# PSUM shared out anew in a fused Fourier and expert kernel: double banks for the Fourier stages, two single banks for the W_in products

## The chip, the cores and the metric

The kernel runs on one core of a Trainium2 chip, as one launch. The metric is device time in microseconds: the median over runs of the whole program, here three of them.

## What is computed

Eight sequences of 3008 tokens with 256 features pass through a Fourier layer and then a wide product layer:

```python
X = np.fft.rfft(x, axis=1)                        # x: 8 x 3008 x 256
Yr = Xr @ w_r - Xi @ w_i + b_r
Yi = Xr @ w_i + Xi @ w_r + b_i                    # w_r, w_i: 256 x 256
Yr, Yi = soft-threshold by 0.01
x = np.fft.irfft(Yr + 1j * Yi, n=3008, axis=1)
h = x @ w_in                                      # w_in: 256 x 2048
out = (h * np.cos(h)) @ w_out                     # w_out: 2048 x 256
```

## The kernel before

The transform over 3008 = 64 x 47 tokens is done as matrix products: `stage_a` multiplies by a 64-point transform, `stage_b` by a 47-point one (`f2t1`), then by the Fourier weights (`wmix`, split into high and low fp32r parts), then `fold` and `spread` go back over the 47 points, and `stage_c` back over the 64 and splits the result into `xTh` and `xTl`. Between stages the data goes through DRAM scratch: `scr1` behind `stage_a`, `scrT` inside `fold`, `scr2` behind `spread`. In `stage_a` (L365) and `spread` (L544) the matmuls are 64x64, four of them to a group, which differ in the 64 rows (`h`) and the 64 columns (`v`) of the array that they use; the two with one `h` write one bank. Such a group is called a quartet below.

The expert layer runs as tiles of 512 tokens, 6 per batch, with 16 steps per tile. A step (`moe_step`) makes a 128x512 block of h with six matmuls into `ph` (L678 to L680), then takes it through a chain: ScalarE rounds h / 2 pi (L685), VectorE subtracts (L686), ScalarE takes the sine (L688), VectorE multiplies by h (L689), ScalarE casts to `gh` (L690), and the rest `gl` is subtracted on GpSimd or VectorE by turns (L267, L270). `ph` is read by L685, L686 and L689. Three steps later `second` multiplies `gh` and `gl` by W_out with six matmuls (L660, L661, L664) into the accumulators `o0` and `o1`.

Batch b's expert steps run beside the Fourier stages of batch b + 1 and `stage_a` of batch b + 2: `moe_step` calls `pull` twice, which draws pieces from these generators according to the costs that they yield (`A_PAIR`, `F2_COST`, and so on). The order in which each engine takes its instructions is then set by a planner that simulates the program as it lays it out; on the chip each engine's order is fixed. Batch 0's Fourier stages run alone ahead of all this, in a prologue that also loads and splits the weights; the splitting of W_out goes on in the first tile.

PSUM has eight banks of 512 fp32 columns. Before, three single banks have the tag `f` (all Fourier work), three the tag `h` (`ph`), and `o0` and `o1` have one each. In the prologue the Fourier stages take turns over all eight.

Of the kernel before, what the change touches and what calls it, by code (L numbers as in the profile page):

```python
# [39 lines left out]
A_EVERY, A_FIRST = 7, 13  # L40
A_PAIR = 1.06
# [99 lines left out]
def tile_body(ctx: ExitStack, tc, x, w_r, w_i, b_r, b_i, w_in, w_out,  # L141
# [78 lines left out]
    def split_f64(hi, lo, raw):  # L220
# [3 lines left out]
        m = wk.tile([128, 512], F32, tag="tr", name="wm", bufs=2)  # L224
# [51 lines left out]
    def fps(name):  # L276
        if "pro" in pool:
            if not banks:
                banks.extend(("f", "h", "o0", "f", "h", "o1", "f", "h"))
            tag = banks.pop(0)  # L280
            return ps.tile([128, 512], F32, tag=tag, name=name, bufs=1 if tag[0] == "o" else 3)
        return ps.tile([128, 512], F32, tag="f", name=name, bufs=3)

    def stage_in(name):
        return wk.tile([128, 512], F32, tag="xt", name=name, bufs=4)

    def stage_out(name):
        return wk.tile([128, 512], F32, tag="ao", name=name, bufs=3)
# [54 lines left out]
    def stage_a(b):  # L343
# [13 lines left out]
        for cc in range(6):  # L357
            for v in range(2):
                load(2 * cc + 2 + v)
            p = [fps("pa") for _ in range(2)]  # L360
            xs = [ld.pop(2 * cc + v) for v in range(2)]
            for v in range(2):
                for h in range(2):
                    hs = slice(64 * h, 64 * h + 64)
                    mm(p[h][64 * v:64 * v + 64], ff[hs, 256:], xs[v][hs], start=True, stop=True, skip_group_check=True)  # L365
            for h in range(2):
                ao = stage_out("ao")
                nc.scalar.copy(ao, p[h])
                for v in range(2):
                    i = 4 * cc + 2 * v  # L370
                    nc.sync.dma_start(scr1[b][:, :, h, i:i + 2].rearrange("s r i d -> (s r) (i d)"), ao[64 * v:64 * v + 64])
            yield A_PAIR


    def stage_b(b):
# [26 lines left out]
        def f2t1(q):  # L402
            if b == 0:
                xf = wk.tile([128, 3, 2, 8, 48], F32, tag=("Xh", "Xl")[q % 2], name="Xf", bufs=1)
                X[q] = xf
            else:
                xh = wk.tile([128, 3, 2, 8, 48], F32R, tag="Xh", name="Xh", bufs=1)
                xl = wk.tile([128, 3, 2, 8, 48], F32R, tag="Xl", name="Xl", bufs=1)
                X[q] = (xh, xl)
            for hf in range(4):  # L410
# [11 lines left out]
                if b:  # L422
                    at = ld.pop(u)
                    p = fps("pb")
# [404 lines left out]
```

## Time and profile before

| | |
|---|---|
| time, median of 3 runs | 2778.85 us (2776.76 to 2781.24) |
| profiled execution, its own time | 2778.31 us |
| its span, first to last instruction | 2776.5 us |
| mean granted TensorE clock | 0.994 |
| busy: TensorE, VectorE, ScalarE, GpSimd | 99%, 65%, 61%, 36% |

The span is what the trace covers; the time of the run has some 1.8 us around it. Busy shares are over the whole span. PE is TensorE, DVE is VectorE, ACT is ScalarE, POOL is GpSimd, SP is SyncE, which issues most of the DMAs.

### The profile page before, as it was taken

To read this page: it belongs to the slowest core of one execution; us is meant where nothing else is said; L and a number is where in the kernel's file an instruction comes from. 1 tells how busy PE (TensorE), PEld (TensorE's weight loads), DVE (VectorE), ACT (ScalarE), POOL (GpSimd) and SP (SyncE) were. 2 spreads that over 40 slices of the span, in tenths; PEclk is the share of its full clock that TensorE was granted. 3 is DMA by queue.
4 is the path that set the end of the run, shared out by engine and by line. 5 is a ranking of instruction groups with operands and counts; after the bars stand their busy time and mean duration, and the time that the engine had idled before them with its cause. 6 is when DMAs were issued, how large, how long until landed. Compare 5 with 4: busy or idle time off the path is not lost.

```text
span 2776.5 us, 36936 instructions
## 1 busy us (share of the span) xinstructions
PE 2741.0 (99%) x13161; PEld 2192.4 (79%) x13161; DVE 1808.6 (65%) x2856; ACT 1690.0 (61%) x3020; POOL 989.6 (36%) x907
## 2 busy tenths in 40 slices
PE   8799999999999999999999999999999999999999
PEld 6487778877788777887778777788777888888888
DVE  6586675766657666676666766667665666666665
ACT  5575556655665655655656555665556656566666
POOL 4354432443324442244322534224442343322222
PEclk9899999999999999999999999999999999999999
DMA  6522333133311433123331233212333122121000
GB/s 188 152 79 73 103 105 91 49 104 111 101 58 54 111 112 101 41 73 107 100 94 42 75 107 105 84 48 73 103 113 92 30 73 88 58 57 38 16 16 15
DMA packets 151193, 224.95 MB, mean 81 GB/s; under 512 B 16976, under 2 KB 94304, under 8 KB 151008
## 3 DMA queue, kind: packets, MB, share of 16 engines
q1 hardware_dynamic: 145728, 205.26, 25.5%
q0 software_dynamic: 5280, 17.33, 2.0%
q8 instruction: 104, 1.70, 0.3%
q14 instruction: 81, 0.66, 0.1%
HBM read 121.33 MB, written 101.19 MB: 80 GB/s over the span
## 4 chain that ended last, share of the span: by engine, by line
PE 93%; DMA 3%; DVE 2%; ACT 0%; SPq 0%; issue 0%; POOL 0%; ACTq 0%; POOLq 0%; DVEq 0%
PE ph L678 12%; PE po L661 12%; PE po L660 12%; PE ph L679 12%; PE ph L680 12%; PE po L664 12%; PE pi L544 3%; PE pb L428 3%; PE pc L641 3%; PE pa L365 2%; PE pw L474 2%; PE pw L473 2%; PE pw L472 2%; DMA y<-scrT 1%; DMA scrT<-tr 1%; PE pw L468 0%
## 5 line engine op out<-in xcount | busy, mean ns | idle before, releaser
L267 POOL TENSOR_TENSOR gl<-u,gh 128x512 fp32r<-128x512 f32 (+1 forms) x384 | 489.1, 1274 | 1301.3 <-ACT gh L690 1086.1
L686 DVE SCALAR_TENSOR_TENSOR u<-ph,u 128x512 f32<-128x512 f32 (+1 forms) x768 | 518.6, 675 | 449.0 <-ACT u L685 447.2
L689 DVE TENSOR_TENSOR u<-ph,u 128x512 f32<-128x512 f32 (+1 forms) x768 | 519.7, 677 | 295.4 <-ACT u L688 279.6
L688 ACT ACTIVATE u<-u 128x512 f32<-128x512 f32 (+1 forms) x768 | 480.1, 625 | 329.1 <-DVE u L686 327.5
L685 ACT ACTIVATE u<-ph 128x512 int32<-128x512 f32 (+1 forms) x768 | 451.2, 588 | 302.1 <-PE ph L680 294.9
L678 PE MATMUL ph<-xTh,win 128*128 128x512 f32 (+1 forms) x1536 | 615.3, 401 | 1.2 <-ACT xTh L645 0.7
L690 ACT CAST gh<-u 128x512 fp32r<-128x512 f32 (+1 forms) x768 | 467.8, 609 | 243.9 <-DVE u L689 242.1
L660 PE MATMUL po<-gh,wout 128*128 128x512 f32 (+1 forms) x1536 | 603.5, 393 | 0.7 <-ACT gh L690 0.7
L661 PE MATMUL po<-gh,wout 128*128 128x512 f32 (+1 forms) x1536 | 599.5, 390 | 0.0
L679 PE MATMUL ph<-xTl,win 128*128 128x512 f32 (+1 forms) x1536 | 597.7, 389 | 0.0
L680 PE MATMUL ph<-xTh,win 128*128 128x512 f32 (+1 forms) x1536 | 597.5, 389 | 0.0
L664 PE MATMUL po<-gl,wout 128*128 128x512 f32 (+1 forms) x1536 | 476.2, 388 | 0.0
L270 DVE TENSOR_TENSOR gl<-u,gh 128x512 fp32r<-128x512 f32 (+1 forms) x384 | 329.4, 858 | 98.3 <-ACT gh L690 95.9
L678 PEld LDWEIGHTS ph<-xTh,win 128*128 128x128 f32 x1536 | 289.8, 189 | 80.2 <-issue 20.3
L661 PEld LDWEIGHTS po<-gh,wout 128*128 128x128 f32 x1536 | 288.9, 188 | 80.9 <-issue 33.3
L660 PEld LDWEIGHTS po<-gh,wout 128*128 128x128 f32 x1536 | 288.9, 188 | 74.5 <-issue 21.9
L680 PEld LDWEIGHTS ph<-xTh,win 128*128 128x128 f32 x1536 | 289.0, 188 | 68.0 <-issue 13.8
L679 PEld LDWEIGHTS ph<-xTl,win 128*128 128x128 f32 x1536 | 289.8, 189 | 65.0 <-issue 19.5
L664 PEld LDWEIGHTS po<-gl,wout 128*128 128x128 f32 x1536 | 285.9, 188 | 58.0 <-issue 3.2
L641 PEld LDWEIGHTS pc<-ff,bt 128*128 128x128 f32 x768 | 112.0, 193 | 24.1 <-issue 13.4
L428 PEld LDWEIGHTS pb<-f,at 96*128 96x128 f32 x896 | 121.0, 191 | 10.3 <-DVE Xl L433 0.2
L641 PE MATMUL pc<-ff,bt 128*128 128x128 f32 x768 | 113.3, 277 | 12.6 <-DMA bt<-scr 12.6
(111 smaller groups left out, 2494.8 us busy)
## 6 DMA issues: line engine op xcount, KB each, us to landing
scrT<-tr SPq DMA_DIRECT2D x56, 512.0 KB, 2.7
y<-scrT SPq DMA_DIRECT2D x112, 256.0 KB, 5.0
bt<-scr SPq DMA_DIRECT2D x96, 256.0 KB, 3.7
xt<-in_dram SPq DMA_DIRECT2D x84, 256.0 KB, 3.2
scr<-ao SPq DMA_DIRECT2D x168, 128.0 KB, 2.9
at<-scr SPq DMA_DIRECT2D x112, 192.0 KB, 2.8
scr<-bo SPq DMA_DIRECT2D x224, 96.0 KB, 2.0
out_dram<-ob SPq DMA_DIRECT2D x80, 256.0 KB, 2.2
```

The source lines that it names most:

```text
L267: return nc.gpsimd.tensor_tensor(out=lo, in0=x, in1=hi.bitcast(F32), op=ALU.subtract)
L660: mm(po[e][:, :n], wo[0][:, 0, f, es], gh[:, :n], start=f == 0, stop=False)
L661: mm(po[e][:, :n], wo[0][:, 1, f, es], gh[:, :n], start=False, stop=False)
L664: mm(po[e][:, :n], wo[0][:, 0, f, es], gl[:, :n], start=False, stop=f == NFC - 1)
L678: mm(h, win[:, 0, c, fs], th[:, c, :n], start=c == 0, stop=False)
L679: mm(h, win[:, 0, c, fs], tl[:, c, :n], start=False, stop=False)
L680: mm(h, win[:, 1, c, fs], th[:, c, :n], start=False, stop=c == 1)
L685: nc.scalar.activation(k[:, :n], h, AF.Identity, bias=0.25, scale=1.0 / TWO_PI)
L686: nc.vector.scalar_tensor_tensor(out=u[:, :n], in0=h, scalar=1.0 / TWO_PI, in1=k[:, :n], op0=ALU.mult, op1=ALU.subtract)
L688: nc.scalar.activation(u[:, :n], u[:, :n], AF.Sin, bias=HALF_PI, scale=TWO_PI)
L689: nc.vector.tensor_tensor(out=u[:, :n], in0=h, in1=u[:, :n], op=ALU.mult)
L690: nc.scalar.copy(gh[:, :n], u[:, :n])
```

## The change

PSUM is divided anew: the tag `f` becomes two tiles of two banks each (`pair`), `h` has two single banks instead of three, `o0` and `o1` stay. In the steady part every Fourier product goes into a pair and is evicted over both banks at once: `stage_a`, `f2t1`, `wmix` (which now makes both halves e of a product together) and `stage_c`; `spread` still copies bank by bank. The four matmuls of a quartet are issued by `burst`, the first with high priority and the others queued directly behind it. `Xh` and `Xl` are laid out so that the wide evictions write in one stretch, and the weights' products read them with gaps. Staging tiles for stores are twice as wide and have half as many DMAs; `xt` has six buffers instead of four, and `tr`, `wm`, `k1`, `cl` (one instead of two) and `yf` (two instead of four) have fewer. In `wmix` both calls of `fold` stand behind the last product. The costs and rates that the generators are drawn by are set to the new pieces.

```diff
 GAP = 5
-A_EVERY, A_FIRST = 7, 13
-A_PAIR = 1.06
+A_EVERY, A_FIRST = 3, 13
+A_PAIR = 1.15
 SPREAD, SPREAD_FIRST = 1.2, 1.1
 
...
         a = wk.tile([128, 512], F32, tag="t2", name="wa", bufs=1)
         q = wk.tile([128, 512], F32, tag="t1", name="wq", bufs=1)
...
+        if not banks:
+            banks.extend(("f", "h", "o0", "f", "h", "o1"))
+        tag = banks.pop(0)
+        if tag == "f":
+            return pair(name)[:, 0]
+        return ps.tile([128, 512], F32, tag=tag, name=name, bufs=1 if tag[0] == "o" else 2)
+
+    def pair(name):
+        return ps.tile([128, 2, 512], F32, tag="f", name=name, bufs=2)
+
+    def burst(calls):
+
+        with tc.high_priority():
+            ins = mm(*calls[0][0], **calls[0][1])
+            with tc.issue_after(ins.ins):
+                for a, k in calls[1:]:
+                    mm(*a, **k)
 
     def stage_in(name):
-        return wk.tile([128, 512], F32, tag="xt", name=name, bufs=4)
+        return wk.tile([128, 512], F32, tag="xt", name=name, bufs=6)
 
     def stage_out(name):
-        return wk.tile([128, 512], F32, tag="ao", name=name, bufs=3)
+        return wk.tile([128, 1024], F32, tag="ao", name=name, bufs=3)
...
         for cc in range(6):
+            p = pair("pa")
+            xs = [ld.pop(2 * cc + v) for v in range(2)]
+            burst([((p[64 * v:64 * v + 64, h], ff[64 * h:64 * h + 64, 256:], xs[v][64 * h:64 * h + 64]),
+                    dict(start=True, stop=True, skip_group_check=True)) for v in (1, 0) for h in range(2)])
+            ao = stage_out("ao")
+            nc.scalar.copy(ao, p.rearrange("p h x -> p (h x)"))
             for v in range(2):
+                i = 4 * cc + 2 * v
+                nc.sync.dma_start(scr1[b][:, :, :, i:i + 2].rearrange("s r g i d -> (s r) g (i d)"),
+                                  ao[64 * v:64 * v + 64].rearrange("p (g x) -> p g x", g=2))
                 load(2 * cc + 2 + v)
-            p = [fps("pa") for _ in range(2)]
-            xs = [ld.pop(2 * cc + v) for v in range(2)]
-            for v in range(2):
-                for h in range(2):
-                    hs = slice(64 * h, 64 * h + 64)
-                    mm(p[h][64 * v:64 * v + 64], ff[hs, 256:], xs[v][hs], start=True, stop=True, skip_group_check=True)
-            for h in range(2):
-                ao = stage_out("ao")
-                nc.scalar.copy(ao, p[h])
-                for v in range(2):
-                    i = 4 * cc + 2 * v
-                    nc.sync.dma_start(scr1[b][:, :, h, i:i + 2].rearrange("s r i d -> (s r) (i d)"), ao[64 * v:64 * v + 64])
             yield A_PAIR
...
-                xh = wk.tile([128, 3, 2, 8, 48], F32R, tag="Xh", name="Xh", bufs=1)
-                xl = wk.tile([128, 3, 2, 8, 48], F32R, tag="Xl", name="Xl", bufs=1)
-                X[q] = (xh, xl)
+                xyh = wk.tile([128, 2304], F32R, tag="Xh", name="Xh", bufs=1)
+                xyl = wk.tile([128, 2304], F32R, tag="Xl", name="Xl", bufs=1)
+                xh, xl = (m[:, :1536].rearrange("p (s g k) -> p s g k", s=8, g=4) for m in (xyh, xyl))
+                yh, yl = (m[:, 1536:].rearrange("p (c s k) -> p c s k", c=2, s=8) for m in (xyh, xyl))
+                X[q] = tuple([[m[:, :, 2 * r + c].rearrange("p s k -> p s k") for c in range(2)] for r in range(2)]
+                             + [[n[:, c] for c in range(2)]] for m, n in ((xh, yh), (xl, yl)))
...
-                    p = fps("pb")
-                    pv = p[:, :384].rearrange("p (s r c k) -> p s r c k", s=2, r=2, c=2)
+                    if hf % 2 == 0:
+                        p = pair("pb")
+                    pv = p[:, hf % 2, :384].rearrange("p (s r c k) -> p s r c k", s=2, r=2, c=2)
                     for j in range(2):
                         for c in range(2):
                             mm(pv[:, j, :, c], at[:, j, 128 * c:128 * c + 128], f2[:, 2 * (hf % 2) + j],
                                start=j == 0 and c == 0, stop=j == 1 and c == 1, skip_group_check=True)
-                    pv = p[:, :384].rearrange("p (s g k) -> p s g k", s=2, g=4)
-                    xhv, xlv = (a[:, :2].rearrange("p r c s k -> p s (r c) k")[:, 2 * hf:2 * hf + 2] for a in (xh, xl))
+                    if hf % 2 == 0:
+                        continue
+                    pv = p[:, :, :384]
+                    xhv, xlv = (a[:, 2 * hf - 2:2 * hf + 2].rearrange("p (u s) g k -> p u (s g k)", u=2) for a in (xh, xl))
                     nc.scalar.copy(xhv, pv)
                     nc.vector.tensor_tensor(out=xlv, in0=pv, in1=xhv.bitcast(F32), op=ALU.subtract)
-                    yield 2 * F2_COST
+                    yield 4 * F2_COST
...
+                (xhr, xhi), (xlr, xli) = ([m.bitcast(F32).rearrange("p s (r c) k -> p r c s k", r=2)[:, r] for r in range(2)]
+                                        for m in (xh, xl))
+                po.tensor_tensor(out=t1, in0=xhr, in1=xhi, op=ALU.add)
+                nc.scalar.copy(yh, t1)
+                po.tensor_tensor(out=t2, in0=xlr, in1=xli, op=ALU.add)
+                po.tensor_tensor(out=t1, in0=t1, in1=yh.bitcast(F32), op=ALU.subtract)
+                po.tensor_tensor(out=yl, in0=t1, in1=t2, op=ALU.add)
...
+            if b:
+                k1 = wk.tile([128, 2, 8, 48], F32, tag="k1", name="k1", bufs=1)
+                for wj, comp in ((0, 2), (1, 0), (2, 1)):
+                    p = pair("pw")
+                    for e in range(2):
+                        es = slice(128 * e, 128 * e + 128)
+                        for c in range(2):
+                            xhv, xlv = (x[comp][c] for x in xs)
+                            mm(p[:, e, :384], wf[:, wj, 0, c, es], xhv, start=c == 0, stop=False)
+                            mm(p[:, e, :384], wf[:, wj, 1, c, es], xhv, start=False, stop=False)
+                            mm(p[:, e, :384], wf[:, wj, 0, c, es], xlv, start=False, stop=c == 1)
+                    p4 = p[:, :, :384].rearrange("p e (s k) -> p e s k", k=48)
+                    if wj == 0:
+                        nc.scalar.copy(k1, p4)
+                        yield 2.0
+                        continue
+                    r = 2 - wj
+                    sv = st[:, :, :, r, :]
+                    if r:
+                        nc.vector.tensor_tensor(out=sv, in0=p4, in1=k1, op=ALU.add)
+                    else:
+                        nc.vector.tensor_tensor(out=sv, in0=k1, in1=p4, op=ALU.subtract)
+                    cl = wk.tile([128, 2, 8, 48], F32, tag="cl", name="cl", bufs=1)
+                    for e in range(2):
+                        nc.vector.tensor_scalar(out=cl[:, e], in0=sv[:, e], scalar1=blo[:, r, e:e + 1],
+                                                scalar2=bhi[:, r, e:e + 1], op0=ALU.max, op1=ALU.min)
+                    nc.vector.tensor_tensor(out=sv, in0=sv, in1=cl, op=ALU.subtract)
+                    yield 2.0
+                for e in range(2):
+                    fold(q, e)
+                return
...
-                k1 = wk.tile([128, 8, 48], F32, tag="k1", name="k1", bufs=2)
+                k1 = wk.tile([128, 8, 48], F32, tag="k1", name="k1", bufs=1)
...
-                        if b == 0:
-                            mm(pv, ws[wj][:, 256 * c + 128 * e:256 * c + 128 * e + 128],
-                               xs[:, comp, c].rearrange("p s k -> p (s k)"), start=c == 0, stop=c == 1)
-                            continue
-                        xhv, xlv = (x[:, comp, c].rearrange("p s k -> p (s k)") for x in xs)
-                        mm(pv, wf[:, wj, 0, c, es], xhv, start=c == 0, stop=False)
-                        mm(pv, wf[:, wj, 1, c, es], xhv, start=False, stop=False)
-                        mm(pv, wf[:, wj, 0, c, es], xlv, start=False, stop=c == 1)
+                        mm(pv, ws[wj][:, 256 * c + 128 * e:256 * c + 128 * e + 128],
+                           xs[:, comp, c].rearrange("p s k -> p (s k)"), start=c == 0, stop=c == 1)
...
-                    cl = wk.tile([128, 8, 48], F32, tag="cl", name="cl", bufs=2)
-                    if b == 0 and q < 3 and r == 0:
+                    cl = wk.tile([128, 8, 48], F32, tag="cl", name="cl", bufs=1)
+                    if q < 3 and r == 0:
...
-                if b:
-                    fold(q, e)
...
-            tr = wk.tile([128, 4, 8, 32], F32, tag="tr", name="tr", bufs=2)
+            tr = wk.tile([128, 4, 8, 32], F32, tag="tr", name="tr", bufs=1)
...
-                p = [fps("pi") for _ in range(2)]
+                p = pair("pi")
+                burst([((p[64 * v:64 * v + 64, h], iw[64 * h:64 * h + 55],
+                         y[64 * h:64 * h + 55, :, 4 * u + 2 * v:4 * u + 2 * v + 2]),
+                        dict(start=True, stop=True, skip_group_check=True)) for v in range(2) for h in (1, 0)])
+                bo = stage_out("bo")
+                for h in range(2):
+                    nc.scalar.copy(bo[:, 512 * h:512 * h + 512].rearrange("p (s a e) -> p s a e", s=2, a=8),
+                                   p[:, h].rearrange("p (a s e) -> p s a e", s=2, a=8))
                 for v in range(2):
-                    for h in range(2):
-                        hs = slice(64 * h, 64 * h + 55)
-                        s0 = 4 * u + 2 * v
-                        mm(p[h][64 * v:64 * v + 64], iw[hs], y[hs, :, s0:s0 + 2], start=True, stop=True,
-                           skip_group_check=True)
-                for h in range(2):
-                    bo = stage_out("bo")
-                    nc.scalar.copy(bo.rearrange("p (s a e) -> p a s e", s=2, a=8),
-                                   p[h].rearrange("p (a s e) -> p a s e", s=2, a=8))
-                    for v in range(2):
-                        s0 = 8 * q + 4 * u + 2 * v
-                        nc.sync.dma_start(scr2[b][:, h, s0:s0 + 2].rearrange("n s d -> n (s d)"), bo[64 * v:64 * v + 48])
+                    s0 = 8 * q + 4 * u + 2 * v
+                    nc.sync.dma_start(scr2[b][:, :, s0:s0 + 2].rearrange("n r s d -> n r (s d)"),
+                                      bo[64 * v:64 * v + 48].rearrange("p (r x) -> p r x", r=2))
                 yield A_PAIR
...
-                y = pool["pro"].tile([128, 512], F32, tag="yf", name="yf", bufs=4)[:96]
+                y = pool["pro"].tile([128, 512], F32, tag="yf", name="yf", bufs=2)[:96]
...
+        p = pair("pc")
         for hf in range(2):
-            p = fps("pc")
             for j in range(2):
                 for c in range(2):
                     o = 256 * j + 128 * c
-                    mm(p[:, o:o + 128], bt[:, 2 * hf + j, 128 * c:128 * c + 128], ff[:, 128:256], start=o == 0, stop=o == 384,
+                    mm(p[:, hf, o:o + 128], bt[:, 2 * hf + j, 128 * c:128 * c + 128], ff[:, 128:256], start=o == 0, stop=o == 384,
                        skip_group_check=True)
-            pv = p.rearrange("p (j c n) -> p c j n", j=2, c=2)
-            thv, tlv = (a[:, :, 256 * hf:256 * hf + 256].rearrange("p c (j n) -> p c j n", j=2) for a in (th, tl))
-            nc.scalar.copy(thv, pv)
-            nc.vector.tensor_tensor(out=tlv, in0=pv, in1=thv.bitcast(F32), op=ALU.subtract)
-            yield 0.86
+        pv = p.rearrange("p f (j c n) -> p c (f j) n", j=2, c=2)
+        thv, tlv = (a.rearrange("p c (i n) -> p c i n", i=4) for a in (th, tl))
+        nc.scalar.copy(thv, pv)
+        nc.vector.tensor_tensor(out=tlv, in0=pv, in1=thv.bitcast(F32), op=ALU.subtract)
+        yield 1.72
...
-        ph = ps.tile([128, 512], F32, tag="h", name="ph", bufs=3)
+        ph = ps.tile([128, 512], F32, tag="h", name="ph", bufs=2)
```

## Rows read from the trace of the kernel before

**Rows 1.** The page's part 1: busy time of each engine, share of the span.

```profile
PE 2741.0 (99%) x13161; PEld 2192.4 (79%) x13161; DVE 1808.6 (65%) x2856; ACT 1690.0 (61%) x3020; POOL 989.6 (36%) x907
```

**Rows 2.** The table of stretches: busy time of each engine in the first two.

```profile
0.00:134.00 134.00, 106.99 (x537) 73.12 (x537) 81.93 (x140) 69.51 (x126) 53.41 (x60) 0.92 0.57 168
134.00:200.00 66.00, 63.77 (x295) 52.54 (x296) 54.10 (x84) 46.33 (x84) 33.53 (x29) 0.93 0.32 90
```

**Rows 3.** TensorE's timeline around two runs of 64x64 matmuls: start, us, engine, line.

```profile
1099.64 0.40 PE L660 MATMUL po<-gh,wout 128*128 128x512 f32 x1
1099.96 1.08 PE L365 MATMUL pa<-xt,ff 64*64 64x512 f32 x4
1100.97 0.50 PE L661 MATMUL po<-gh,wout 128*128 128x512 f32 x1
...
927.66 0.39 PE L679 MATMUL ph<-xTl,win 128*128 128x512 f32 x1
927.89 0.39 PE L680 MATMUL ph<-xTh,win 128*128 128x512 f32 x1
928.21 1.09 PE L365 MATMUL pa<-xt,ff 64*64 64x512 f32 x8
929.23 0.50 PE L660 MATMUL po<-gh,wout 128*128 128x512 f32 x1
```

**Rows 4.** Groups by line and form: records, busy us and mean ns, idle before.

```profile
L365 PE MATMUL pa<-xt,ff 64*64 64x512 f32 x336 | 75.3, 614 | 0.0
...
L544 PE MATMUL pi<-y,iw 55*64 55x512 f32 x448 | 105.6, 614 | 1.5 <-DMA y<-scrT 1.5
```

**Rows 5.** The timeline of TensorE and VectorE over a clean step of products.

```profile
839.57 0.39 PE L678 MATMUL ph<-xTh,win 128*128 128x512 f32 x1
...
843.21 0.69 DVE L689 TENSOR_TENSOR u<-ph,u 128x512 f32<-128x512 f32 x1
...
845.51 0.39 PE L678 MATMUL ph<-xTh,win 128*128 128x512 f32 x1
```

**Rows 6.** The timeline of GpSimd and VectorE where a remainder is held.

```profile
852.50 1.85 POOL L450 TENSOR_TENSOR t<-Xh 128x768 f32<-128x768 f32 x1
...
856.12 1.83 POOL L453 TENSOR_TENSOR t<-t,Xh 128x768 f32<-128x768 f32 x1
...
853.30 5.20 DVE L270 TENSOR_TENSOR gl<-u,gh 128x512 fp32r<-128x512 f32 x1 [0.69 <-ACT gh L690]
```

**Rows 7.** L270's group by form, and its line's durations (min/median/max ns).

```profile
L270 DVE TENSOR_TENSOR gl<-u,gh 128x512 fp32r<-128x512 f32 x320 | 289.8, 906 | 88.6 <-ACT gh L690 87.0
...
L270 DVE TENSOR_TENSOR gl<-u,gh x384: 615/684/5204, 153.3 to 2770.0; 128x512 fp32r<-128x512 f32 x160, 128x448 fp32r<-128x448 f32 x32
```

**Rows 8.** The timeline of TensorE and VectorE in the first tile.

```profile
150.40 0.39 PE L678 MATMUL ph<-xTh,win 128*128 128x512 f32 x1
...
156.20 1.47 DVE L689 TENSOR_TENSOR u<-ph,u 128x512 f32<-128x512 f32 x2
```

**Rows 9.** The group of a cast of 768 columns on ScalarE.

```profile
L451 ACT CAST Xh<-t 128x768 fp32r<-128x768 f32 x28 | 23.3, 832 | 1.9 <-POOL t L450 1.9
```

**Rows 10.** The chain that ended last, at the prologue's end: start, us, what.

```profile
122.48 2.51 DMA scr<-ao
...
126.88 0.65 SPq L633
...
127.58 6.68 DMA bt<-scr
```

**Rows 11.** The same chain at a batch's first quarter of stage B.

```profile
559.33 3.80 DMA scrT<-tr
...
564.48 6.01 DMA y<-scrT
```

**Rows 12.** TensorE's timeline in the Fourier weights' products.

```profile
930.72 0.34 PE L472 MATMUL pw<-Xh,wf 128*128 128x384 f32 x1
930.89 0.35 PE L473 MATMUL pw<-Xh,wf 128*128 128x384 f32 x1
```

More of the change, by code (lines that the diff above doesn't have):

```diff
@@ L223, in split_f64 @@
         v = pair[:, :, 1]
-        m = wk.tile([128, 512], F32, tag="tr", name="wm", bufs=2)
+        m = wk.tile([128, 512], F32, tag="tr", name="wm", bufs=1)
         a = wk.tile([128, 512], F32, tag="t2", name="wa", bufs=1)
@@ L276, in fps @@
     def fps(name):
[L277 to L282, printed above, removed]
+        if not banks:
[12 more added lines that the diff above has]
+                    mm(*a, **k)
     def stage_in(name):
-        return wk.tile([128, 512], F32, tag="xt", name=name, bufs=4)
+        return wk.tile([128, 512], F32, tag="xt", name=name, bufs=6)
     def stage_out(name):
-        return wk.tile([128, 512], F32, tag="ao", name=name, bufs=3)
+        return wk.tile([128, 1024], F32, tag="ao", name=name, bufs=3)
     def beside(*gens):
@@ L449, in f2t1 @@
                 po = nc.gpsimd
-                po.tensor_tensor(out=t1, in0=xh[:, 0].bitcast(F32), in1=xh[:, 1].bitcast(F32), op=ALU.add)
-                nc.scalar.copy(xh[:, 2], t1)
-                po.tensor_tensor(out=t2, in0=xl[:, 0].bitcast(F32), in1=xl[:, 1].bitcast(F32), op=ALU.add)
-                po.tensor_tensor(out=t1, in0=t1, in1=xh[:, 2].bitcast(F32), op=ALU.subtract)
-                po.tensor_tensor(out=xl[:, 2], in0=t1, in1=t2, op=ALU.add)
+                (xhr, xhi), (xlr, xli) = ([m.bitcast(F32).rearrange("p s (r c) k -> p r c s k", r=2)[:, r] for r in range(2)]
[5 more added lines that the diff above has]
+                po.tensor_tensor(out=yl, in0=t1, in1=t2, op=ALU.add)
         def wmix(q):
@@ L494, in wmix @@
                                             op0=ALU.max, op1=ALU.min)
-                    (nc.gpsimd if b == 0 and q < 3 else nc.vector).tensor_tensor(out=sv, in0=sv, in1=cl, op=ALU.subtract)
+                    (nc.gpsimd if q < 3 else nc.vector).tensor_tensor(out=sv, in0=sv, in1=cl, op=ALU.subtract)
                     yield 1.0
-                if b:
-                    fold(q, e)
         Y = {}
@@ L584, in idft @@
                        skip_group_check=True)
-                bo = stage_out("bo")[:96]
+                bo = stage_out("bo")[:96, :512]
                 nc.scalar.copy(bo, p[:96])
```

## The prediction

> **What bounds the kernel now.** Read the page's first part first: TensorE is busy for 2741.0 of 2776.5 us, and no other engine is above 65% [rows 1]. A share like that can hide waits, because a pipelined matmul looks busy while it waits, so the second view is the table of stretches: of the 35.5 us in which TensorE idles, 27.0 lie in the prologue (134.00 less 106.99) and 2.2 in the first tile of products (66.00 less 63.77) [rows 2]. The 2,576 us behind them hold 6 us of idle time. So in the long middle the sum of TensorE's issue steps is the time: whatever shortens that sum shortens the kernel, and whatever makes TensorE wait lengthens it.
>
> The third view, TensorE's timeline, shows a step of 0.23 us from a 512-column product to the next (927.66 to 927.89), and one thing that costs far more: a run of 64x64 matmuls. The run of four records at 1099.96 stands between products that start at 1099.64 and 1100.97; 1.33 us less the ordinary 0.23 is 1.10 us for the run. A run of eight records (928.21) stands between 927.89 and 929.23: 1.34 less 0.23, 1.11 us, for twice the work [rows 3]. Each fp32 matmul of the code stands as two records here: `stage_a` writes 7 batches x 6 x 4 = 168 of them and the trace has 336 [rows 4]. So eight records are one full quartet, and four are half of one, at the same price.
>
> **What the pinned quartets save.** A run is busy for 1.08 us, short or long [rows 3], so the groups of L365 and L544 tell how many runs there are: 75.3 / 1.08 = 70 and 105.6 / 1.08 = 98 [rows 4], 168 together. The code has 42 quartets in `stage_a` and 7 x 4 x 2 = 56 in `spread`, 98 together. Some 70 quartets are thus split today: their two banks are separate tiles of the ring `f`, and the two matmuls into one bank may run long before the other two. The change gives a quartet one tile of two banks, so that nothing but its inputs can part it, and queues its last three matmuls behind its first. 168 runs become 98: 70 x 1.10 = **77 us less**. The bounds are 0 (the quartets stay parted) and 77; I take 77, since a run of eight is a row and no guess.
>
> **What the wider evictions save.** One 128x768 cast takes 0.83 us (L451) where two of 128x384 are replaced [rows 9]; ScalarE and VectorE do a few us less in all, and they are at 61% and 65% [rows 1]. On the path that sets the end this is nothing, as TensorE's products hide it; without that cover a quartet's eviction would show in full. The halved number of scratch stores is likewise hidden on SP, except at one place below. The weights' products now stream `Xh` and `Xl` in runs of 48 with gaps: nothing by the nearest row, because L544 streams `y` in pieces and its run takes the same 1.08 us by the quotient above; should gaps halve the rate, 672 products of 0.17 us each (930.72 to 930.89) [rows 12] would cost 114 us. I take 0, and keep that as a rival.
>
> The Trainium skill speaks against quartets: "TensorEngine Tiling (Array Packing)", under Performance Considerations, "PSUM Bottleneck", says that tiling speeds up TensorE and not the emptying of PSUM, which may then be the bound. Taken at its word, each quartet's 1.1 us would come back as a wait for ScalarE, and the 77 us would be gone; ScalarE at 61% says otherwise in this trace.
>
> **What two banks for W_in's products cost.** `ph` is held from its first matmul until L689 has multiplied it. In a clean step the first matmul starts at 839.57, L689 ends at 843.21 + 0.69 = 843.90, and the step after next starts at 845.51 [rows 5]: with two banks instead of three that step could still start on time, with 1.6 us to spare. The slack is used up where VectorE is held. At 853.30 a remainder (L270) takes 5.20 us instead of 0.68, from the time that GpSimd starts three operations at 852.50 until the third ends at 856.12 + 1.83 = 857.95 [rows 6]. Behind it on VectorE wait L686 and L689 of the steps in flight, so their banks stay full; today the third bank carries TensorE over it. Over the whole kernel the 320 wide remainders have a mean of 0.906 us against a median of 0.684 [rows 7]: 320 x 0.22 = 71 us of holding. That is the upper bound, 0 the lower. The longest loses 4.5 - 1.6 = 2.9 of its 4.5 us, shorter ones a smaller share or nothing, and the planner can put Fourier matmuls in the gap. I take a little over a quarter, **20 us more**.
>
> On that holding the Trainium skill ("SBUF — State Buffer", "Who interferes with whom") says that a VectorE instruction with two SBUF inputs and a GpSimd one that reads SBUF exclude each other, the later waiting until the first finishes. By one GpSimd instruction (1.85 us in the rows) a holding would be nearly within the slack and the term near 0; the row shows a holding through three in a row, so the row's sum stands.
>
> **The prologue and the first tile.** `fps` now deals out 6 banks instead of 8, `yf` 2 buffers instead of 4, and `wm`, `k1` and `cl` one instead of two, so there is less lead there. Of the 27.0 us idle in the prologue [rows 2], 6.68 is its last load (127.58) [rows 10]; the other 20 are waits on buffers and loads. Bounds: nothing, and those 20 once more; I take **6 more**, nearer to nothing because TensorE's lead is cut by a quarter and not taken away. At the prologue's end something is won: the chain of waits shows `bt` issued at 126.88 because SP stands behind scratch stores of `ao`, and the last of these behind a buffer that a store starting at 122.48 frees 2.51 us later [rows 10]. With one wide `ao` per quartet in a ring of three that wait goes: **4 less** (bounds 0 and 4, from 122.9 to 126.9). The first `stage_c` is evicted in one piece behind all its matmuls instead of in halves: **1 more**. In the first tile the splitting of W_out loads VectorE: a step that starts at 150.40 is multiplied only at 156.20 + 1.47 = 157.67, 7.3 us later [rows 8]. Three banks allow a step each 7.3 / 3 = 2.4 us, two each 3.6; over 16 steps at most 19 us, and less since steps there are limited by more than banks: **6 more** (0 to 10; the longest hold is not every step's).
>
> **What the late fold costs.** Both halves of `fold` now follow the last weight product, and the second half's transposes wait for the one `tr` buffer, whose store takes 3.80 us to land (559.33). Then come 6.01 us of the load of `y` (564.48) [rows 11]. I estimate `y` later by about that landing, 3.8 us, since the second half no longer has a buffer of its own. TensorE has products to do in the meantime, and has waited 1.5 us in all for `y` [rows 4]; the planner places the quartet after the load. I take 0; the upper bound stands with the rivals.
>
> **Sum.** The profiled execution took 2778.3 us (span 2776.5 and 1.8 around it), 0.5 below the median of the three runs, which is nothing. 2778.3 - 77 + 20 + 6 - 4 + 1 + 6 = 2730. With every bound at its best 2697, at its worst 2778 - 77 + 71 + 20 + 1 + 10 = 2803. A change of 0.2% (5.6 us) is about what a measurement of this kernel can tell.
>
> **The rivals.**
> 1. The slack of two banks is enough everywhere, or the new order keeps VectorE out of GpSimd's way: no 20, little in the prologue; 2697 to 2710. For it: pure products leave 1.6 us. Against it: seven us of hold in the first tile.
> 2. The other side, slower: GpSimd's three operations stop the two-bank pipeline in every quarter. Place: VectorE's queue behind an L270 that meets them; price: 857.95 - 852.50 = 5.45 less 1.6, 3.9 us each; 28 quarters give 109 us, and the sum is 2730 - 20 + 109 = 2819. It decides from 17 of 28 on (17 x 3.9 = 66, which with the other terms eats the 77). For it: the third bank hides several today. Against it: the mean says that most L270 miss the three operations.
> 3. The fold's 3.8 us show in the first quarter of each batch, where the chain of waits already passes through `y` [rows 11]: 7 x 3.8 = 27 us, 2757. At all 28 quarters it would be 106, 2836.
> 4. The quartets stay parted or run one pair at a time in the new order: 2730 + 77 = 2807.
> 5. Gaps in the moving operand cost 114: 2844.
> 6. ScalarE becomes the bound behind quartets: each needs two copies of 0.58, some 1.1 us; only if every quartet waited for its own would 77 come back, 2807. ScalarE's 39% of idle time speaks against it, and I give it no more than quartets that stay parted.
>
> **Chances.** The forecast with its spread (2715 to 2755) 0.47; rival 1 0.26; rival 2 0.11; rival 3 0.08, most of it at 2757; rivals 4 and 6 together 0.05; rival 5 0.03. Faster by over 0.2% is the forecast, rival 1 and six in eight of rival 3: 0.79. Within 0.2% are the partial forms of rivals 2 and 3: 0.05; slower 0.16. The range from 2697 to 2790 leaves out some 0.05 below and 0.13 above. The likeliest case alone spans 2715 to 2755.
>
> **What would show it.** In the changed profile L365's matmuls should be busy for about 42 x 1.08 = 45 us and `pi`'s for 56 x 1.08 = 60, all in runs of eight between neighbours 1.34 apart; if the runs of four stay, the first step is wrong. TensorE's idle time behind 200 us should be near 20, with the waits of `ph` on L689 the new row and long L270 at the same place; waits on `y` near 2 us; the weights' products still 0.17 apart. The prologue should end a few us later or earlier than 134, not twenty. The prediction is wrong if `ph` waits on L689 for over 60 us, or if any eviction of a Fourier pair appears as what TensorE waits for.

## The result and the profile after

The changed kernel takes 2754.23 us (median of 4 runs, 2752.36 to 2756.97) beside 2780.05 us for the kernel before on the same chip (4 runs): ratio 0.9906, 95% interval 0.9887 to 0.9925. That is 26 us faster; the forecast was 48. The profiled execution has a span of 2751.6 us, 24.9 less than before.

The page's first part and the first two stretches of the table of stretches, for the changed kernel, answer to [rows 1, 2]:

```profile
PE 2673.5 (97%) x13161; PEld 2186.7 (79%) x13161; DVE 1763.5 (64%) x2640; ACT 1670.5 (61%) x2846; POOL 988.7 (36%) x907
...
0.00:134.00 134.00, 106.19 (x540) 71.60 (x541) 81.32 (x141) 69.36 (x121) 51.76 (x60) 0.94 0.58 170
134.00:200.00 66.00, 56.73 (x257) 43.62 (x257) 53.86 (x69) 39.56 (x69) 36.04 (x30) 0.94 0.34 93
```

TensorE is busy 67.5 us less (2741.0 to 2673.5) and idle 42.6 us more (35.5 to 78.1). So most of a large gain was made, and more than half of it was given back as waits. Of the 78.1 us of idle time 27.8 lie in the prologue (before 27.0), 9.3 in the stretch of the first tile (2.2), and 41.0 behind it (6).

The gain, in the groups by line and form. L290 is the first matmul of a quartet, L293 the other three; the two overlap, so their times are not added. They answer to [rows 4]:

```profile
L293 PE MATMUL pi<-y,iw 55*64 55x512 f32 x336 | 62.5, 624 | 0.0
...
L290 PE MATMUL pi<-y,iw 55*64 55x512 f32 x112 | 60.4, 621 | 18.5 <-DMA y<-scrT 18.5
...
L293 PE MATMUL pa<-xt,ff 64*64 64x512 f32 x252 | 46.3, 614 | 0.0
...
L290 PE MATMUL pa<-xt,ff 64*64 64x512 f32 x84 | 44.9, 614 | 1.1 <-DVE Xl L447 1.1
```

Where 75.3 and 105.6 us stood, some 46 and 62 stand: 42 and 56 quartets of 1.1 us, none of them parted. Each run taken as in [rows 3], from the last start ahead of it to the first start behind it, less the ordinary 0.23 us and less the waits, the runs of the whole trace sum to 188.1 us before (167 runs, 133 of them of four records) and to 112.8 us now (94 runs of eight records and 2 of sixteen, two quartets in a row): 75.3 less ("quartet time" below). In the same rows stands the first of the losses: 18.5 us of waiting for `y`, where [rows 4] have 1.5.

The table of what TensorE waited for (us in total, times, longest):

```profile
PE pc L677 <- DMA bt<-scr: 25.4, 8, 11.4
PE pi L290 <- DMA y<-scrT: 18.5, 12, 3.7
PE ph L714 <- DVE u L725: 5.7, 8, 1.6
PE po L700 <- DVE gl L270: 4.2, 4, 1.2
```

The longest wait on `bt` is that at the prologue's end. The other seven are one per batch, 14.0 us together. With 17.0 more on `y` they make 31 of the 35 us that TensorE idles more behind the first tile. The wait that the prediction had put its 20 us on, `ph` behind VectorE, is 5.7 us, and 4.0 of them lie in the first tile.

Two of these waits in the chain that ended last (start, us, what):

```profile
1039.36 2.60 DMA scrT<-tr
...
1043.53 2.60 DMA scrT<-tr
...
1047.74 5.56 DMA y<-scrT
...
1053.44 0.61 PE pi L290
...
1067.61 4.18 DMA bt<-scr
...
1071.93 1.80 PE pc L677 x14
```

And the timeline of SyncE's queue (SP) between them:

```profile
1055.80 8.78 SPq L587 DMA_DIRECT2D scr<-bo  x4
1066.95 1.27 SPq L669 DMA_DIRECT2D bt<-scr  x2
```

They hang together. The last quarter's `pi` waits for `y`; its four stores of `bo` follow; and the next batch's `bt` is the load of what they store, so it is issued only once they have landed.

A wait also costs something behind it. In the table of stretches, the one behind the wait on `bt` that ended at 1732.2 us, and the next (the last three numbers are the granted clock, the DMA share and GB/s):

```profile
1732.90:1736.30 3.40, 3.40 (x14) 3.05 (x13) 0.69 (x1) 0.30 (x1) 0.00 (x0) 0.50 0.00 0
1736.30:1740.00 3.70, 3.70 (x18) 3.05 (x17) 0.69 (x1) 0.60 (x1) 0.00 (x0) 1.00 0.35 89
```

TensorE is busy throughout both, but in the first the granted clock is at the lower of its two levels (1.2 GHz, a share of 0.50), and there a 512-column product takes 0.43 us instead of 0.23 (from 2184.30 to 2184.73 in one such stretch, from 2187.57 to 2187.80 behind it). Between the first tile and the end six such stretches, 24 us together, stand in the changed kernel, each at or just behind the end of a wait of 1.8 to 3.7 us on `y` or `bt`; not every such wait has one. The kernel before has one, of 3.4 us, behind its longest wait on `y`. At half the clock these stretches cost, as an estimate, 24 / 2 - 3.4 / 2 = 10 us more than before, which stand in TensorE's busy time and not among the waits.

The first tile, in the timeline of TensorE and VectorE (matmuls of `ph` and the last reader of `ph`), answers to [rows 8]:

```profile
145.88 0.50 PE L714 MATMUL ph<-xTh,win 128*128 128x512 f32 x1 [0.76 <-DVE u L725]
...
148.47 0.50 PE L714 MATMUL ph<-xTh,win 128*128 128x512 f32 x1
...
154.04 0.68 DVE L725 TENSOR_TENSOR u<-ph,u 128x512 f32<-128x512 f32 x1
...
154.78 0.50 PE L714 MATMUL ph<-xTh,win 128*128 128x512 f32 x1
...
157.29 0.68 DVE L725 TENSOR_TENSOR u<-ph,u 128x512 f32<-128x512 f32 x1
...
158.31 0.39 PE L714 MATMUL ph<-xTh,win 128*128 128x512 f32 x1
...
163.07 0.69 DVE L725 TENSOR_TENSOR u<-ph,u 128x512 f32<-128x512 f32 x1
...
163.82 0.50 PE L714 MATMUL ph<-xTh,win 128*128 128x512 f32 x1 [1.26 <-DVE u L725]
```

A step here starts 0.06 to 0.34 us behind the end of L725 of the step two before (154.78 behind 154.72, 158.31 behind 157.97, 163.82 behind 163.76). The two banks set the pace: each is held for 8.8 to 9.5 us. From the first step's start to the seventeenth's the tile takes 62.7 us (138.2 to 201.0); before it took 51.3 (138.8 to 190.1).

### The profile page after: what moved, and what is told of

It is laid out like the page before. It is cut to its first block, busy times and chain, and to the rows that moved or that the text cites. A ratio compares the mean times of both kernels' runs of the same rounds, so it can differ in the third digit from the quotient of the medians.

```text
span 2751.6 us, 36096 instructions
## 1 busy us (share of the span) xinstructions
PE 2673.5 (97%) x13161; PEld 2186.7 (79%) x13161; DVE 1763.5 (64%) x2640; ACT 1670.5 (61%) x2846; POOL 988.7 (36%) x907
## 4 chain that ended last, share of the span: by engine, by line
PE 81%; DMA 8%; DVE 6%; issue 2%; ACT 1%; POOL 1%; SPq 1%; ACTq 0%; DVEq 0%; POOLq 0%
PE po L696 11%; PE ph L714 11%; PE po L700 11%; PE ph L715 11%; PE ph L716 11%; PE po L697 11%; PE pc L677 3%; DMA scrT<-tr 3%; DMA y<-scrT 3%; PE pb L440 3%; PE pw L486 2%; PE pw L485 2%; PE pw L484 2%; PE pi L290 2%; PE pa L290 1%
## 5 line engine op out<-in xcount | busy, mean ns | idle before, releaser
L725 DVE TENSOR_TENSOR u<-ph,u 128x512 f32<-128x512 f32 (+1 forms) x768 | 520.2, 677 | 262.4 <-ACT u L724 245.4
L700 PE MATMUL po<-gl,wout 128*128 128x512 f32 (+1 forms) x1536 | 482.2, 392 | 4.4 <-DVE gl L270 4.2
L270 DVE TENSOR_TENSOR gl<-u,gh 128x512 fp32r<-128x512 f32 (+1 forms) x384 | 310.1, 808 | 52.3 <-ACT gh L726 45.7
L677 PEld LDWEIGHTS pc<-ff,bt 128*128 128x128 f32 x768 | 105.5, 200 | 36.2 <-issue 17.9
```

What stands on the lines that cost most here:

```text
L700: mm(po[e][:, :n], wo[0][:, 0, f, es], gl[:, :n], start=False, stop=f == NFC - 1)
L725: nc.vector.tensor_tensor(out=u[:, :n], in0=h, in1=u[:, :n], op=ALU.mult)
```

## The experiments

All were timed beside the kernel before on the same chip; ratios are to it. After a first reading of the trace, theory A said that the double bank is what joins a quartet, and that what is given back is the price of the third `ph` bank. The rival said that the late fold delays `y`. (In the expectations of the two runs with an earlier fold the letters stand the other way: there A is the late fold, and B the banks.) Theories C and D came later and are told where they come in.

**One half of the gain alone.** The kernel before, with the helper `burst` but single banks:

```diff
+            burst([((p[h][64 * v:64 * v + 64], ff[64 * h:64 * h + 64, 256:], xs[v][64 * h:64 * h + 64]),
+                    dict(start=True, stop=True, skip_group_check=True)) for v in (1, 0) for h in range(2)])
...
+                burst([((p[h][64 * v:64 * v + 64], iw[64 * h:64 * h + 55],
```

> The kernel before with the quartets' four matmuls issued by the new helper, the banks as they were (three single ones for the Fourier stages, three for ph). Theory A (the double bank is what joins a quartet): its two single banks come free at different times, so the four stay parted; the 64x64 lines stay busy for about 75 and 105 us and the time is 2760 to 2785. Theory B (the queueing behind the first matmul is what joins them): the lines fall to about 46 and 61 us and the time to about 2705.

Measured: 2773.39 us, 0.9984 (0.9975 to 0.9993). Its groups by line and form (L287 is the first matmul here, L290 the others):

```profile
L290 PE MATMUL pi<-y,iw 55*64 55x512 f32 x336 | 103.9, 610 | 0.0
...
L290 PE MATMUL pa<-xt,ff 64*64 64x512 f32 x252 | 82.9, 612 | 0.0
...
L287 PE MATMUL pi<-y,iw 55*64 55x512 f32 x112 | 56.2, 604 | 7.1 <-DMA y<-scrT 6.9
...
L287 PE MATMUL pa<-xt,ff 64*64 64x512 f32 x84 | 44.7, 614 | 1.9 <-ACT bo L589 1.9
```

L290 is busy for 103.9 and 82.9 us, far from the 62 and 46 of whole quartets; quartet time is 180.3 us (188.1 before). Queueing the four behind each other joins next to nothing while their two banks are separate tiles. A holds.

**The third `ph` bank alone.** The kernel before with two `ph` banks and four single `f` banks:

```diff
-        return ps.tile([128, 512], F32, tag="f", name=name, bufs=3)
+        return ps.tile([128, 512], F32, tag="f", name=name, bufs=4)
...
-        ph = ps.tile([128, 512], F32, tag="h", name="ph", bufs=3)
+        ph = ps.tile([128, 512], F32, tag="h", name="ph", bufs=2)
```

> The kernel before with two banks for ph instead of three; the freed bank goes to the Fourier stages as a fourth single one. Theory A (two banks cost something only where VectorE and ScalarE split W_out): the first tile takes some 11 us more, the batches behind it the same as before; 2780 to 2795. Theory B (what GpSimd holds back on VectorE reaches TensorE everywhere): waits of ph on L689 in every batch, 4 us a batch or more, 2800 to 2840.

Measured: 2823.81 us, 1.0162 (1.0147 to 1.0177), above A's 2780 to 2795 and inside B's 2800 to 2840. But B's waits did not come: those of `ph` on L689 are 4.0 us in all. The first tile grows by 9.5 us to 60.8, and with `fold` untouched the table of waits has a new wait on `y`, and behind the prologue's 12.1 us on `bt` another 3.5, nearly all in one wait:

```profile
PE pc L641 <- DMA bt<-scr: 15.6, 3, 12.1
PE pi L544 <- DMA y<-scrT: 12.7, 14, 2.2
...
PE ph L678 <- DVE u L689: 4.0, 4, 1.3
```

But quartets part further as well (quartet time 205.1 us, 17 more than before), so the 46 us are not the price of the bank alone.

**The late fold undone, in two ways.** First `wmix` again makes one half after the other, with `fold` behind each and `k1` and `cl` in two buffers (and `A_EVERY` 5 instead of 3); then `tr` and `wm` get their second buffers back (paid for by `xt`, four instead of six):

```diff
+                for e in range(2):
+                    es = slice(128 * e, 128 * e + 128)
...
+                        pv = pair("pw")[:, 0, :384]
...
+                    fold(q, e)
```

> The changed kernel with wmix as before: the halves e one after the other, each product in one bank of a pair, each half's fold right behind it, k1 and cl with two buffers. Theory A (the late fold is what is paid back: y lands late, quartets and their stores with it, and bt stands behind those stores on SP): TensorE's waits on y fall from 18.5 us to under 6, those on bt behind the prologue from 14 to under 5, the time to 2720 to 2738. Theory B (these waits come from a TensorE that is earlier, or from the banks of ph): they stay, and the time is 2748 to 2760.

```diff
-            tr = wk.tile([128, 4, 8, 32], F32, tag="tr", name="tr", bufs=1)
+            tr = wk.tile([128, 4, 8, 32], F32, tag="tr", name="tr", bufs=2)
...
-        return wk.tile([128, 512], F32, tag="xt", name=name, bufs=6)
+        return wk.tile([128, 512], F32, tag="xt", name=name, bufs=4)
```

> The changed kernel with two buffers for tr and wm (and four for xt instead of six, to make the room). Theory A (the late fold): VectorE no longer waits for the store of tr (28.2 us in the changed kernel), y lands some 2.6 us earlier, and about half of the waits on y and bt goes: 2735 to 2748. Theory B: VectorE's waits for the store go, TensorE's waits stay, 2748 to 2760.

Measured: 2770.26 us, 0.9975 (0.9966 to 0.9985), and 2779.45 us, 1.0002 (0.9991 to 1.0013); both slower than the change, and than either theory had put them. Waits on `y`, from the table of waits of the first and then of the second:

```profile
PE pi L290 <- DMA y<-scrT: 25.0, 12, 3.5
```

```profile
PE pc L677 <- DMA bt<-scr: 30.5, 14, 11.6
PE pi L290 <- DMA y<-scrT: 16.1, 11, 2.3
PE pb L440 <- DMA at<-scr: 12.2, 5, 3.3
```

An earlier fold does not take the waits away, nor does the second buffer. (The fewer `xt` bring a new one, on `at`.) Behind the prologue those on `bt` are 16.2 and 18.9 us, not less than the change's 14.0. The late fold falls.

**Priority and distance.** Theory C: a quartet issued with high priority comes too early, before its `y`. Tested by taking the priority from `burst`, and by giving the planner more distance ahead of the last `spread` and of `pc`:

```diff
-        with tc.high_priority():
-            ins = mm(*calls[0][0], **calls[0][1])
+        ins = mm(*calls[0][0], **calls[0][1])
```

> The changed kernel without the high priority of a quartet's first matmul; the other three are still queued behind it. Theory C (the high priority puts a quartet right where the planner has y landing, and on the chip y lands later): TensorE's waits on y fall from 19 us to under 6; in the order as built some 28 of the 98 quartets are parted again, 1.1 to 2.2 us each, so the 64x64 matmuls take 30 to 60 us more than in the changed kernel, and the time is 2755 to 2795. Theory D (the waits come from having two banks for ph, which leaves TensorE fewer products at hand): the waits on y stay near 19 us.

```diff
-        yield 2.0
+        yield 8.0
         yield from inverse(3)
...
-        yield 3.5
+        yield 6.5
         p = pair("pc")
```

> The changed kernel with more of the products drawn ahead of two waits: 8.0 instead of 2.0 of cost before the last quarter's spread and 6.5 instead of 3.5 between the load of bt and the matmuls on it, and the rates adjusted to that. Theory C (the planner's landings are early, so a little distance covers them): TensorE's waits on bt behind the prologue fall from 15 us to under 4, those on y by a third, the time to 2728 to 2742. Theory D (two banks for ph): the waits only move, 2748 to 2758.

Measured: 2785.26 us, 1.0025 (1.0015 to 1.0035), and 2766.25 us, 0.9951 (0.9935 to 0.9966). Waits on `y`, and for the first on `bt` (its longest is the prologue's), in the tables of the two:

```profile
PE pi L289 <- DMA y<-scrT: 15.6, 11, 3.4
PE pc L676 <- DMA bt<-scr: 15.2, 4, 11.5
```

```profile
PE pi L290 <- DMA y<-scrT: 26.9, 16, 3.7
```

Without priority `y` is waited for nearly as long, and the quartets part again (quartet time 162.8 us): in this version with two double banks the priority does hold them together. So one tile for a quartet is needed, but does not by itself keep it whole. More distance makes it worse, and slower than D had it, too. For `y` C falls. For `bt` it does not quite: without priority the waits on `bt` behind the prologue fall from 14.0 to 3.7 us, so a large part of those hangs on the priority as well as on the banks.

**The gain without the loss.** Theory D: the waits on `y` and `bt` come with two `ph` banks, however the Fourier work is arranged. So: the kernel before with three `ph` banks, its Fourier stages on one double bank `f` and one single bank `g` by turns, and quartets always in the double bank, pinned; once with high priority, once without:

```diff
+        turns.append(0)
+        if len(turns) % 2:
+            return ps.tile([128, 512], F32, tag="g", name=name, bufs=1)
+        return pair(name)[:, 0]
+
+    def pair(name):
+        return ps.tile([128, 2, 512], F32, tag="f", name=name, bufs=1)
...
+            pp = pair("pa")
+            p = [pp[:, h] for h in range(2)]
```

> The kernel before with three banks for ph as it had, and the Fourier stages on one double bank and one single one: quartets take the double bank and are issued by the new helper with high priority, all else takes the single bank and half of the double one by turns; evictions, folds and loads as before. Theory C: the 64x64 matmuls take 104 us as in the changed kernel, the first tile 51 us as before, waits on y are still 10 to 20 us; 2715 to 2730. Theory D: waits on y and bt are as small as before (2 us), 2698 to 2712. If three banks are too few for the Fourier stages, waits of their matmuls on evictions show, and the time is above 2730.

> The same without the high priority. Theory C: all quartets still whole (104 us), waits on y under 6 us, first tile 51 us; 2698 to 2712, faster than both kernels. Theory D: no different from the run with high priority. If three banks are too few, as there.

Measured: 2699.60 us, 0.9714 (0.9699 to 0.9728), and 2700.38 us, 0.9712 (0.9697 to 0.9726). Groups by form and the table of waits of the one without priority:

```profile
L297 PE MATMUL pi<-y,iw 55*64 55x512 f32 x336 | 60.6, 614 | 0.0
L294 PE MATMUL pi<-y,iw 55*64 55x512 f32 x112 | 59.8, 614 | 1.3 <-DMA y<-scrT 0.9 <-issue 0.4
```

```profile
PE pc L653 <- DMA bt<-scr: 9.9, 1, 9.9
PE pb L455 <- ACT at L404: 4.7, 2, 2.6
```

Quartets are whole (109.3 us), the waits on `y` and `bt` are gone but for the prologue's and 0.9 us, and the first tile takes 51.7 us. This beats the kernel before by 78 us and the change, which was timed on another chip, by some 54, with none of the wider evictions.

Then the same kernel with two `ph` banks and two `g`, and the changed kernel with three `ph` banks and one double bank:

```diff
-            return ps.tile([128, 512], F32, tag="g", name=name, bufs=1)
+            return ps.tile([128, 512], F32, tag="g", name=name, bufs=2)
...
-        ph = ps.tile([128, 512], F32, tag="h", name="ph", bufs=3)
+        ph = ps.tile([128, 512], F32, tag="h", name="ph", bufs=2)
```

> The kernel of the last run (three banks for ph, one double bank and one single one for the Fourier stages, no high priority) with one bank moved: two for ph, two single ones beside the double bank. All else as there. Theory D (the third bank of ph is what keeps TensorE off y, bt and the first tile's waits): waits of TensorE on y, bt and ph together rise by 20 to 50 us, the first tile takes some 9 us more, 2722 to 2755. Theory E (the wide evictions and the late fold of the change make those waits, together with its high priority): they stay small here, only the first tile is longer, 2704 to 2715.

```diff
-        return ps.tile([128, 2, 512], F32, tag="f", name=name, bufs=2)
+        return ps.tile([128, 2, 512], F32, tag="f", name=name, bufs=1)
...
-        ph = ps.tile([128, 512], F32, tag="h", name="ph", bufs=2)
+        ph = ps.tile([128, 512], F32, tag="h", name="ph", bufs=3)
```

> The changed kernel with one bank moved the other way: three for ph, one double bank instead of two for the Fourier stages in the steady part (the eighth bank is used in the prologue alone); wide evictions, late fold, single tr buffer and high priority as changed. Theory D: waits on y and bt are under 6 us in all, the first tile 52 us, 2698 to 2715, unless one double bank is too few, which would show as waits of Fourier matmuls on evictions. Theory E: waits on y and bt stay at 30 us, about 2740.

Measured: 2791.56 us, 1.0045 (1.0029 to 1.0062), and 2736.46 us, 0.9849 (0.9835 to 0.9864). The tables of waits, of the first and then of the second:

```profile
PE pi L294 <- DMA y<-scrT: 25.8, 14, 3.7
PE pc L653 <- DMA bt<-scr: 16.8, 12, 9.8
```

```profile
PE pc L677 <- DMA bt<-scr: 11.7, 5, 9.4
PE pc L677 <- ACT wm L236: 11.3, 1, 11.3
PE ph L714 <- ACT xTh L681: 8.8, 8, 1.1
PE ph L714 <- DVE u L725: 7.4, 7, 1.4
```

And what `pc` waited for in the second between 300 and 600 us:

```profile
  DMA bt<-scr: 9.4, 1
```

Taking the third bank away brings both waits back and lengthens the first tile from 51.7 to 58.3 us; giving it to the changed kernel takes that on `y` away (1.1 us are left) and shortens the tile from 62.7 to 49.7. Both of these signs are D's. With `bt` it is less clear: its seven waits of about 2 us, one per batch, go (four of 2.3 us together are left), but a single one of 9.4 us comes at 489 us, so that behind the prologue 11.7 us stand against 14.0. Neither time lies where D had put it. The first is slower than forecast: its prologue is 8 us longer, some quartets part (quartet time 127.7 us), `po` waits 8.9 us for `gl`, and the mean granted clock of the profiled execution is 0.987 against 0.995 in the kernel with the third bank. The second gains less than forecast, and its 2736 us is E's "about 2740", though the waits that E named are not there: besides the 9.4 us, its two rows of `ph` sum to 16.2 us, against 6.8 in the change. That its one double bank, with the wide evictions, is behind these was not tried apart. (The wait of `pc` on `wm` lies in the prologue, which ends 0.6 us later than before.)

**Why `y` is waited for.** Counted from the traces, with no run: the W_in and W_out products that TensorE has between a quarter's last weights' product and its first matmul of `pi`, the time between the starts of the two, and, behind "lands", when the last load of `y` has landed in that time. A block is the Fourier work of one batch beside the products of the one before it; there are seven. "Steady" is the second to the sixth, "last" the seventh.

```
                  last quarter, steady                                     last block, quarters 0 to 2
before            57 products, 14.5 us, lands 13.7 to 14.3                 56, 60, 55 products
after             90 products, 22.0 to 22.4 us, lands 21.8 to 22.3         74, 70, 68 products
third `ph` bank   99 products, 22.0 to 23.1 us, lands 21.1 to 23.0         90, 87, 84 products
more distance     78 products, 20.8 to 21.2 us, lands 20.7 to 21.0         74, 70, 82 products
fold undone       56 products, 16.5 to 17.9 us, lands 16.4 to 17.7         60, 60, 60 products
```

("Third `ph` bank" is the changed kernel with one double bank; "fold undone" the one with `wmix` as before.) In the last quarter TensorE starts `pi` after the same 22 us, with 90 products and a wait of 0.6 to 1.1 us each time, or with 99 and, but for one wait of 0.7 us, none. With two banks `y` lands 0.4 us later than with three on the mean of the five, from 0.7 earlier to 1.0 later, and TensorE has nine products, about 2 us, less laid out ahead of it. Beside the kernel before, `y` does land later in the changed kernel, by 8 us, but the planner lays 90 products there instead of 57; and where the fold is undone `y` lands 5 us earlier, with only 56 products ahead, and is waited for all the same. The other waits on `y` of the change (2.2, 1.8, 3.7, 3.0 and 1.5 us) stand where 68 to 76 products are laid, in the first and the last block. More distance dealt the products anew, more to quarter 0 and fewer to the others, and the waits followed.

## Why the prediction was right in sign and half off in size

**Quartets, 77 us less: right.** Quartet time fell by 75.3 us, the quartets are whole, and `pa` and `pi` are busy for about 45 and 60 us as forecast. The first experiment shows that queueing alone does not do it; the two-bank tile is needed, and in the changed kernel the priority too. The Trainium skill's "PSUM Bottleneck" ("TensorEngine Tiling (Array Packing)"), by which the emptying of PSUM may become the bound, did not come true here: no wait of TensorE behind a quartet's eviction is among the four largest, and ScalarE stayed at 61%. The prediction had called itself wrong if any eviction of a Fourier pair was waited for. One was, once, for 1.1 us (`Xl` at L447, in the rows of the result): too little to matter, so the sign was set too fine.

**Wider evictions and gaps at nothing: right.** The weights' products, in the groups by form of the changed kernel:

```profile
L484 PE MATMUL pw<-Xh,wf 128*128 128x384 f32 x336 | 114.7, 341 | 0.0
...
L485 PE MATMUL pw<-Xh,wf 128*128 128x384 f32 x336 | 113.5, 338 | 0.0
```

At 341 and 338 ns they stand where the products of [rows 12] stand (0.34 and 0.35 us), and their steps have a median of 0.175 us. Rival 5 is out.

**Two `ph` banks, 20 us more: the step that failed.** I sized it by VectorE held at L270, and put the cost into waits of `ph` on VectorE. Its group and its line (min/median/max ns) answer to [rows 7]:

```profile
L270 DVE TENSOR_TENSOR gl<-u,gh 128x512 fp32r<-128x512 f32 x320 | 262.3, 820 | 50.9 <-ACT gh L726 45.0 <-PE pw L486 2.1
...
L270 DVE TENSOR_TENSOR gl<-u,gh x384: 615/684/3861, 150.4 to 2745.1; 128x512 fp32r<-128x512 f32 x160, 128x448 fp32r<-128x448 f32 x32
```

The holdings shrank (mean 906 to 820 ns, longest 5.2 to 3.9 us) and `ph` waits on VectorE for 5.7 us, 1.7 of them behind the first tile. Rival 2 is out too. The price of two banks was paid elsewhere: 31 us of waits on `y` and `bt`, with some 10 us of lower clock behind them, for which the prediction had no term. All seven kernels with two banks wait 12.7 to 26.9 us for `y`; the kernels with three wait 0 to 1.5, and 6.9 where single banks are pinned. For the 14 us on `bt` the priority of the quartets counts too, as said above. Why the planner lays fewer products ahead when `ph` has two banks was only argued: its simulation may hold a step back until a bank is free, and fill that place with Fourier work.

**The first tile, 6 more: right in kind, too small.** It was 11.4, above my bound of 10. I took a hold of 7.3 us from [rows 8]; in the steps shown it was 8.8 to 9.5 us, and at two banks that paces them.

**The prologue, 6 more, less 4, 1 more: near in sum, by luck.** The first `ph` starts at 138.2 us instead of 138.8, where the three terms make 3 more. From the chain of the changed kernel:

```profile
122.34 3.71 DMA scr<-bo
...
126.13 0.62 SPq L669
```

`bt` is issued at 126.13 instead of 126.88, so 0.75 us were won and not 4: SP no longer stands behind the buffer of `ao`, but behind a store of `bo`. From the first `pc` to the first `ph` it takes 4.9 us instead of 4.4, half of the 1 forecast. So next to nothing is left for the 6: the two larger terms were both too large and cancel.

**The late fold at nothing: right, though the wait I named came.** Rival 3 gave 2757 us, near the result, for the wrong reason: `y` is waited for, but undoing the late fold in two ways does not help. `y` lands some 8 us later in the last quarter, not 3.8, and the planner lays products ahead of it, as the prediction said it would. The forecast that waits on `y` would stay near 2 us was wrong.

In sum, -75 for the quartets, +43 of idle time (31 on `y` and `bt`, 7 in the stretch of the first tile, 5 the rest), about +10 for the lower clock and -2 for what is left make the -25 of the two spans. That 2754 us still lies in the likeliest case, at its edge of 2755, is luck: the large gain was read rightly, and the losses came from other places than the ones that were added up.

## What to carry to other kernels

Of the groups of four small matmuls that share the array most were parted here as long as their banks were separate tiles. Queueing them was not enough, and in two of the versions one tile for all their banks was not either, so count the runs in the trace. Before a bank is taken from a pipeline for this, ask whether the packed work can do with less: one double and one single bank gave the whole gain here at next to no price. And where a planner lays out the order, fewer buffers also change what it lays ahead of a load, so a wait can appear at a load that lands hardly later than it would with more buffers. A wait of TensorE can cost more than its own length: look at the granted clock behind it.

## What was not expected of the hardware

The wide remainders on VectorE were held for less in the changed kernel (longest 3.9 us, before 5.2), though GpSimd's busy time is the same (988.7 and 989.6 us) [rows 1, 7]; which GpSimd operations they meet was not looked into.
